# Zeros for the first products, a split first load, and one inverse on VectorE instead of through DRAM

## The chip, the core and the metric

The kernel runs on one NeuronCore of a Trainium2 chip. Its engines are TensorE (PE; its weight loads are listed apart, as PEld), VectorE (DVE), ScalarE (ACT), GpSimd (POOL) and SyncE (SP), which here issues all DMAs. The metric is the time of one execution on the device in microseconds, the median of several runs.

## The reference

Attention with capped scores over 4 batch entries of 12 heads (448 tokens, 64 features per head), then a layer norm and two feed-forward blocks:

```python
scores = cap * np.tanh(scale * (q @ k.T) / cap)
attn = np.exp(scores - scores.max(-1)); attn /= attn.sum(-1) + 1e-09
x = attn @ v                                # to [4, 448, 768]
xn = (x - mu) / np.sqrt(var + 1e-06) * g_ln
x = x + np.maximum(xn @ w_ch1, 0.0) @ w_ch2 # 768 -> 3072 -> 768
h = np.maximum(x @ w_in, 0.0); u, v = h[..., :512], h[..., 512:]
out = (u * (w_spatial @ norm(v) + b_spatial)) @ w_out
```

All is float32. The change touches only the attention of the first two batch entries.

## The kernel before

Every operation is recorded first. `Recorder` notes engine, a cost and a latency from a small table, and the call (line 560; the call itself is line 561, so almost every instruction of the profile bears L561). `Program.order` derives due times from TensorE's own order, and `Program.plan` is a list scheduler: it runs the recorded operations against those costs, gives out the buffers of the pools, and lets ScalarE take some of VectorE's copies where that is earlier. What it puts out is, for each engine, one fixed list, and each engine works through its list in order. So an operation that waits holds up all behind it on its engine, and SyncE's list holds up every DMA behind one that waits.

Heads are worked in pairs, named by the first head: pair i is heads i and i + 1 of the 48. The lead phase is the 12 pairs 0 to 22 of entries 0 and 1. For one pair:

- `emit_load(i)` loads `qk`, 128 rows (64 features of two heads) by 896: 448 query columns, then 448 key columns. There are two such buffers, so pair i + 4 is loaded over pair i.
- `lead_s(i)` makes three products of 128 keys by 448 queries into PSUM (`two`, `two`, `t3`), and ScalarE the tanh of each (scale `qsc`, made from the loaded `cap`) and the exponentials `e`. `lead_st(i)` does the last 64 keys of two pairs at once.
- `lead_v(i)` adds the exponentials up on VectorE (`es`), multiplies `e` with the values `vt` on TensorE into a `bank` of PSUM (there are only two in this phase), copies the result to `x`, and makes the row sums with products by ones (`onesr`, `sel`) in a bank.
- The row sums are inverted. `invert` (line 1001) takes a copy of them, writes it to DRAM (`sum`), reads it back spread over 128 rows (`rc`), inverts that on VectorE, writes it to DRAM (`inv`) and broadcasts it to a tile `hs` by two or four DMAs. For a pair named in `FAST` (line 938), VectorE inverts the bank directly, in four pieces of 112 columns. Pairs 8, 10, 20 and 22 have sums of their own; the others share them by two, and their DMAs bear the number of the second.
- `emit_n(i)` multiplies `x` by the inverse and `x_done` adds it to `acc`. After pair 10, the last of entry 0, `ln_mean` needs `acc`: a product `bank<-wh,onesr` for the mean over features.

Beside this, four rows of the first weight matrix are made ready (`make`): they are loaded as 64-bit words (`w`), put together by four operations into `wr`, split into two parts for the later products (`rs`, `wh`), and written to DRAM (`kept_w`).

Ahead of the recorded list TensorE multiplies zeros with zeros, into a bank that nothing reads.

Of the kernel before, what the change touches and what calls it, by code (L numbers as in the profile page):

```python
# [10 lines left out]
F32 = mybir.dt.float32  # L11
# [29 lines left out]
LN_AT = 4.2  # L41
MAKE = 3.1

FAST = 22,

COUNTS = 16, 10, 3, 2, 3, 1
FIRST = 2, 2, 2, 1
# [521 lines left out]
def attn_ffn_gmlp_kernel(  # L569
# [15 lines left out]
    nc = tc.nc  # L585
    prog = Program(nc)
    V, A, P, T, SP = (prog.engines[n] for n in ("V", "A", "P", "PE", "D"))
    B, H = qk.shape[0], qk.shape[1]
    KD, S = out.shape[1], out.shape[3]
# [70 lines left out]
    for stage in four, mid:  # L660
# [4 lines left out]
    xts = [[const.tile([128, S], F32, name=f"x{i}_{k}") for k in range(KD)] for i in range(2)]  # L665
# [3 lines left out]
    capt = const.tile([128, 1], F32, name="capt")  # L669
# [6 lines left out]
    banks = Slots("bank", [psum.tile([128, 512], F32, name=f"bank{i}") for i in range(2)],  # L676
                  late=[Later(f"bank{i}", [128, 512], F32) for i in range(2, 4)])
# [144 lines left out]
    def emit_load(i):  # L822

        if i >= len(heads):
            return
        b, h = heads[i]
        t = raws[i] = qks.get()

        SP.dma_start(out=t, in_=qk[b, h:h + 2].rearrange("a p n -> (a p) n")[64:192])

    def place(i):


        return slice(64, 128) if i // 2 % 2 else slice(0, 64)

    def emit_load_v(i):


        if i >= len(heads):
            return  # L840
        b, h = heads[i]
        u = raws["v", i] = vts[i // 2 % 2].get()
        p = place(i)
        SP.dma_start(out=u[:, 0:384].rearrange("p (a n) -> p a n", a=2),
                     in_=v[b, h:h + 2, :, 0:3].rearrange("a p c d -> p a (c d)"))
        SP.dma_start(out=u[p, 384:512].rearrange("p (a n) -> p a n", a=2),
                     in_=v[b, h:h + 2, p, 3].rearrange("a p d -> p a d"))
# [58 lines left out]
    def lead_v(i):  # L906
# [30 lines left out]
        R = [hs.get() for _ in now]  # L937
        if i in FAST:

# [104 lines left out]
    def emit_v(i, ns=range(4)):  # L1044
# [41 lines left out]
        R = [hs.get() for _ in now]  # L1086
        if i in FAST:

# [348 lines left out]
    def gmlp(bs, nxt):  # L1437
        for b in nxt:
            ln_load(b)
        if not last_pass[0]:  # L1440
            for i in range(1, KH):
                ahead("wu", i)
        vs = v_mm(range(2 * S // 128))
        for b in nxt:
            ln_mean(b)
        if last_pass[0]:
            mix_y()
            u_four(bs, 0)
            v_norm(vs)
            u_four(bs, 1)  # L1450
        else:
            u_units(bs, 0)
            v_norm(vs)
            for i in range(1, KH):
                for k in range(max(2 * i - 2, 0), 2 * i):
                    ahead("wo", k)
                u_units(bs, i)
        ysp.clear()
        sp = spatial()
        with prog.early():  # L1460
            for b in nxt:
                centre(b)
        for b in nxt:
            scale(b)
        bias = xts[0][KD - 1] if last_pass[0] else bsg.get()
        SP.dma_start(out=bias, in_=b_sp)
        for i in range(0, KH, 2):
            sp_pair(bs, (i, i + 1), sp, bias)
            if i + 2 == KH:
                with prog.early():  # L1470
                    for b in nxt:
                        normalise(b)
        us.clear()
        vn.clear()
        if last_pass[0]:
            o_four(bs)
            gs.clear()
            return
        for dts in ([0, 1, 2], *([dt] for dt in range(3, KD))):
            w = [weight("wo", dt) for dt in dts]  # L1480
            for b in bs:
                if b % 2:
                    for dt, x in zip(dts, w):
                        o_units(b, dt, [x])
                else:
                    o_units(b, dts[0], w)
        gs.clear()
        if nxt:
            for k in range(KD // 2):
                mix(k)  # L1490
        for b in nxt:
            ln_load(b)
# [209 lines left out]
    def second_pass(bs):  # L1702
        hidden.clear()
        for i in range(NF // 2):
            h_four(i)
        y_seven(wq, wq)
# [120 lines left out]
    def drive(units, todo):  # L1827

        todo = deque(sorted(todo, key=lambda t: t[0]))
        spent = 0  # L1830
        for n in units:
            spent += n
            while todo and todo[0][0] < spent:
                _, fn, args = todo.popleft()
                fn(*args)
        for _, fn, args in todo:
            fn(*args)

    def attend(first, n, per):
        todo = []  # L1840
        for j in range(0, n, 2):
            i = first + j
            t = per * j

            stages = [(S_AT[0] if i >= 2 * SPLIT else 0.0, emit_s, i, (0, 1)),
                      (S_AT[1] if i >= 2 * SPLIT else 0.1, emit_s, i, (2,)), (LOAD_QK, emit_load, i + 4),
                      (LOAD, emit_load_v, i + 2)]
            if i < 2 * H:

                stages = [(0.0, lead_s, i), (2.05, lead_v, i)] + stages[2:]  # L1850
            else:
                stages += [(2.05, emit_v, i)]
            if i // 2 % 2 == 0:
                stages += [(LEAD_ST, lead_st, i) if i < 2 * H else (ST, emit_st, i)]
            if alone(i):
                stages += [(4.2, emit_n, i)]
            elif i // 2 % 2:
                stages += [(4.2, emit_n, i - 2), (4.2, emit_n, i)]
            todo += [(t + x * per, fn, a) for x, fn, *a in stages]
        return todo  # L1860

    def main():
        with prog.at_once():
            emit_load(0)
            SP.dma_start(out=capt, in_=cap)
            emit_load(2)
            emit_load_v(0)
        SP.dma_start(out=g_t, in_=g_ln)
        P.memset(sel, 0.0)
        for j in (0, 2):  # L1870
            P.memset(sel[place(j), j // 2], 1.0)
        P.memset(ones32, 1.0)
        V.tensor_copy(onesr, ones32[:, 0:1].broadcast_to([128, 128]))
        P.memset(mhalf, -0.5)
        V.reciprocal(qsc, capt)
        V.tensor_scalar(out=qsc, in0=qsc, scalar1=float(D) ** -0.5, scalar2=None, op0=ALU.mult)

        lead = attend(0, 2 * H, 1.0) + [(x, fn, (b,)) for x, b in ((H + LN_AT, 0), (2 * H + 2.25, 1)) for fn in (ln_mean, ln_center)]
        lead += [(MAKE + j * H / EARLY, make, ("w1", j)) for j in range(EARLY)]
        drive([], lead)  # L1880
        for p in range(NP):
            bs = 2 * p, 2 * p + 1

            if p:
                last_pass[0] = True
                second_pass(bs)
                gmlp(bs, [])
                continue
            total = NF * 2 * 3 * KD
            rows = [("w2", (q, g)) for q in (BLOCKS[0], BLOCKS[2]) for g in range(NG)]  # L1890
            later = [("wv", k) for k in range(KD)] + [("wu", i) for i in range(1)] + [("wo", k) for k in range(0)]
            todo = [(total * (AFTER[0] + (AFTER[1] - AFTER[0]) * j / len(rows)), ahead, x) for j, x in enumerate(rows)]
            n = 2 * H
            drive(h_units(bs), todo + attend(n, n, AFTER[2] * total / n))
            raw6[:] = w6m, wcm, w6m
            y_seven(wqm, wqs, later)
            raw6[:] = w6g, wcg, w6g
            gmlp(bs, [2 * p + 2, 2 * p + 3])

    main()  # L1900
    tops.begin()
    att.begin()
# [4 lines left out]
    with tc.manual_schedule():  # L1907
        t = tok_t[0][0]
        nc.vector.memset(t[:], 0.0)
        nc.scalar.activation(out=t[:], in_=t[:], func=ACTF.Tanh)  # L1910
        t = xts[0][0]
        nc.vector.memset(t[:], 0.0)
        for _ in range(2):
            nc.tensor.matmul(out=banks.tiles[-1][:, 0:S], lhsT=t[:, 0:128], rhs=t[:], start=True, stop=True)
        prog.issue()


# [52 lines left out]
```

## Time and profile before

| | |
|---|---|
| runs | 1012.73, 1012.03, 1009.84 us; median 1012.03 |
| profiled execution | 1010.37 us, its span 1008.6 us |
| TensorE busy | 997.3 us (99%), 5108 instructions |
| VectorE busy | 855.2 us (85%) |
| ScalarE busy | 584.9 us (58%) |
| granted TensorE clock | 1.0 over the span |

The profile is one execution. Times in it count from the span's start. An engine's row gives, in brackets, how long the engine was idle just before and what ended that; a matmul's end is modelled, and a DMA's row on SyncE is its issue, not its transfer. SyncE's name in rows is SPq.

### The profile page before, as it was taken

What the parts mean: (1) busy time and instruction counts of PE and PEld (TensorE: products, weight loads), DVE (VectorE), ACT (ScalarE), POOL (GpSimd) and SP (SyncE); (2) the same over time, 40 slices, a digit from 0 to 9 for tenths busy, and PEclk for the clock granted to TensorE, in tenths of its full rate; (3) what the DMA queues carried; (4) which work ended last, traced back from release to release, by engine and by line L of the source; (5) the groups of instructions that cost most, each with busy time, mean ns of one, the idle gap of its engine ahead of it and who ended that gap; (6) DMA issues with size and microseconds to landing.
All of it is one profiled execution on the core that took longest, in us unless ns stands there. A gap on an engine that the chain in (4) does not pass through costs nothing.

```text
span 1008.6 us, 14721 instructions
## 1 busy us (share of the span) xinstructions
PE 997.3 (99%) x5108; PEld 827.7 (82%) x5108; DVE 855.2 (85%) x1425; ACT 584.9 (58%) x890; POOL 16.7 (2%) x22
## 2 busy tenths in 40 slices
PE   8999999999999999999999999999999999999998
PEld 2334787787788899998989889999999999998987
DVE  6767887888967899989889999877788988968996
ACT  7996955877775358656356355444453543314653
POOL 0000000000000000000000200000000000000010
PEclk9999999999999999999999999999999999999999
DMA  7546678988897998997386233565699857302402
GB/s 251 170 137 180 214 254 294 365 305 303 300 331 230 347 359 297 332 345 273 119 308 218 43 144 116 169 204 191 236 329 371 290 184 233 103 21 71 128 21 110
DMA packets 121197, 224.30 MB, mean 222 GB/s; under 512 B 20594, under 2 KB 83236, under 8 KB 121124
## 3 DMA queue, kind: packets, MB, share of 16 engines
q1 hardware_dynamic: 121124, 223.38, 65.1%
q8 instruction: 40, 0.66, 0.3%
q14 instruction: 33, 0.27, 0.1%
HBM read 152.76 MB, written 70.57 MB: 221 GB/s over the span
## 4 chain that ended last, share of the span: by engine, by line
PE 84%; DMA 6%; DVE 6%; issue 1%; ACT 1%; SPq 1%; DVEq 0%; ACTq 0%
PE bank L561 58%; PE two L561 26%; DMA w6m<-in_w_dram 2%; DVE rs L561 1%; DVE x L561 1%; DMA hs<-inv 1%; DMA std<-var_t 1%; DVE wh L561 1%; DMA w<-in_w_dram 1%; SPq L561 1%; PE t L561 1%; DVE qkg L561 1%; DMA wq<-kept_w 1%; DMA qk<-in_qk_dram 1%; DVE wr L561 1%
## 5 line engine op out<-in xcount | busy, mean ns | idle before, releaser
L561 PE MATMUL bank<-rs,wh 128*128 128x448 f32 x1728 | 362.9, 363 | 1.2 <-DVE rs L561 0.7
L561 PEld LDWEIGHTS bank<-rs,wh 128*128 128x128 f32 x1728 | 322.5, 187 | 29.5 <-issue 3.0
L561 PE MATMUL two<-rs,wh 128*128 128x448 f32 x462 | 103.7, 362 | 0.7 <-DVE wh L561 0.7
L561 DVE TENSOR_TENSOR rs<-hs,rs 128x448 fp32r<-128x448 f32 x159 | 94.3, 618 | 4.7 <-ACT rs L561 4.5
L561 ACT ACTIVATE rs<-hs 128x448 fp32r<-128x448 f32 x135 | 73.2, 570 | 32.7 <-DMA hs<-h 31.4
L561 PEld LDWEIGHTS two<-rs,wh 128*128 128x128 f32 x462 | 86.5, 187 | 6.9 <-DVE wh L561 1.0
L561 DVE TENSOR_TENSOR wh<-wr,wh 128x768 fp32r<-128x768 f32 (+2 forms) x66 | 57.4, 871 | 3.0 <-ACT wh L561 2.5
L561 ACT ACTIVATE hs<-bank 128x448 f32<-128x448 f32 x58 | 31.5, 543 | 40.1 <-PE bank L561 33.9
L561 ACT ACTIVATE wh<-wr 128x768 fp32r<-128x768 f32 (+2 forms) x44 | 33.7, 766 | 30.8 <-PE bank L561 16.6
L561 ACT ACTIVATE es<-es,capt 128x896 f32<-128x896 f32 x42 | 42.6, 1052 | 0.1
L561 ACT ACTIVATE hx<-bank 128x448 f32<-128x448 f32 x30 | 16.3, 543 | 39.2 <-PE bank L561 30.1
L561 PE MATMUL two<-qk 64*128 64x448 f32 (+1 forms) x168 | 36.1, 575 | 2.9 <-DMA qk<-in_qk_dram 2.0
L561 ACT ACTIVATE rs<-x 128x448 fp32r<-128x448 f32 x29 | 16.3, 575 | 36.5 <-DVE x L561 35.1
L561 PE MATMUL bank<-es,vt 128*64 128x448 f32 (+1 forms) x192 | 36.0, 551 | 0.0
L561 ACT ACTIVATE es<-two,qsc 128x896 f32<-128x896 f32 x32 | 31.5, 1007 | 6.3 <-PE two L561 6.3
L561 PE MATMUL two<-wh,rs 128*128 128x512 f32 x144 | 34.7, 389 | 0.0
L561 PE MATMUL bank<-rx,whb 128*128 128x448 f32 x144 | 32.7, 362 | 0.0
L561 PE MATMUL two<-rx,whb 128*128 128x448 f32 x144 | 32.7, 362 | 0.0
L561 DVE TENSOR_TENSOR es<-es,es 128x896 f32<-128x896 f32 x24 | 26.1, 1086 | 7.5 <-ACT es L561 7.5
L561 PEld LDWEIGHTS two<-qk 64*128 64x128 f32 (+1 forms) x168 | 11.3, 173 | 25.5 <-issue 9.1
L561 PEld LDWEIGHTS two<-wh,rs 128*128 128x128 f32 x144 | 27.0, 188 | 5.6
L561 ACT ACTIVATE e<-e,capt 128x2688 f32<-128x2688 f32 (+1 forms) x14 | 31.0, 2224 | 0.2
(268 smaller groups left out, 1966.1 us busy)
## 6 DMA issues: line engine op xcount, KB each, us to landing
hs<-h SPq DMA_DIRECT2D x168, 224.0 KB
h<-hx SPq DMA_DIRECT2D x84, 224.0 KB
w<-in_w_dram SPq DMA_DIRECT2D x24, 768.0 KB
qk<-in_qk_dram SPq DMA_DIRECT2D x24, 448.0 KB
h<-hs SPq DMA_DIRECT2D x48, 224.0 KB
kept_w<-wr SPq DMA_DIRECT2D x24, 384.0 KB
w6q<-in_w_dram SPq DMA_DIRECT2D x12, 768.0 KB
w6m<-in_w_dram SPq DMA_DIRECT2D x12, 768.0 KB
```

The source lines that it names most:

```text
L561: fn(*(put(a) for a in args), **{k: put(a) for k, a in kw.items()})
```

## The change

`FAST` names pair 10 too, so its row sums are inverted on VectorE, in four pieces, and its five DMAs, the copy and the small reciprocal are gone. The first `qk` tile comes in two DMAs, the queries with the first 128 keys and then the other keys, with `cap` between them. The products of zeros read a constant of the runtime's that GpSimd fills before the program's start, in place of a tile that VectorE set to zero; a third product of 112 columns follows the two of 448.

```diff
-FAST = 22,
+FAST = 10, 22
...
-        SP.dma_start(out=t, in_=qk[b, h:h + 2].rearrange("a p n -> (a p) n")[64:192])
+        x = qk[b, h:h + 2].rearrange("a p n -> (a p) n")[64:192]
+        for r in (slice(0, S + 128), slice(S + 128, 2 * S)) if i == 0 else (slice(0, 2 * S),):
+            SP.dma_start(out=t[:, r], in_=x[:, r])
+            if r.start == 0 and i == 0:
+                SP.dma_start(out=capt, in_=cap)
...
             emit_load(0)
-            SP.dma_start(out=capt, in_=cap)
             emit_load(2)
...
-        t = xts[0][0]
-        nc.vector.memset(t[:], 0.0)
-        for _ in range(2):
-            nc.tensor.matmul(out=banks.tiles[-1][:, 0:S], lhsT=t[:, 0:128], rhs=t[:], start=True, stop=True)
+        zeros = nc.const_aps.tensor(0.0, [128, S], F32)
+        for n in (S, S, S // 4):
+            nc.tensor.matmul(out=banks.tiles[-1][:, 0:n], lhsT=zeros[:, 0:128], rhs=zeros[:, 0:n], start=True, stop=True)
```

The planner then orders the lists anew. TensorE's list stays the same but for the zeros; those of VectorE, ScalarE and SyncE differ in places up to the layer norm of entry 0, and are the same after it. (Numbers at the end of a name are tile numbers, which shift by two after the change.)

In SyncE's list the load of the keys of pair 6 and the third weight load change places, so that the keys go first. Pair 10's five DMAs are gone from it.

VectorE at the additions for pair 2 (`es_434<-e_420` before, `es_432<-e_418` after). Before:

```order
L561 TENSOR_SCALAR wr_92<-w_424 128x768
L561 CAST rs_65<-wr_93 128x768
L561 TENSOR_TENSOR es_434<-e_420 128x896
L561 TENSOR_TENSOR rs_66<-wr_93,rs_65 128x768
L561 TENSOR_TENSOR es_434<-es_434,e_420 128x896
L561 COPY x_1_114<-bank_139 128x448
```

and after:

```order
L561 TENSOR_SCALAR wr_92<-w_422 128x768
L561 TENSOR_TENSOR es_432<-e_418 128x896
L561 CAST rs_65<-wr_93 128x768
L561 TENSOR_TENSOR es_432<-es_432,e_418 128x896
L561 TENSOR_TENSOR rs_66<-wr_93,rs_65 128x768
L561 COPY x_1_114<-bank_139 128x448
```

The subtraction into `rs_66` moved behind the second addition.

SyncE behind the last write of a prepared weight row, `kept_w_3` (the sums and inverses of pairs 0 and 2 bear a 2, those of 4 and 6 a 6). Before:

```order
L561 DMA sum_2_143<-hs_79 4x448
L561 DMA vt_0_415<-in_v_dram 64x2x64
L561 DMA vt_0_415<-in_v_dram 128x2x192
L561 DMA rc_89<-sum_2_143 128x14
L561 DMA qk_412<-in_qk_dram 128x896
L561 DMA sum_6_146<-hs_80 4x448
L561 DMA inv_2_144<-rc_89 128x14
L561 DMA qk_413<-in_qk_dram 128x896
L561 DMA rc_90<-sum_6_146 128x14
L561 DMA hs_79<-inv_2_144 64x448 x2
L561 DMA hs_81<-inv_2_144 64x448 x2
L561 DMA inv_6_147<-rc_90 128x14
```

and after, behind the same write:

```order
L561 DMA vt_0_413<-in_v_dram 64x2x64
L561 DMA vt_0_413<-in_v_dram 128x2x192
L561 DMA sum_2_143<-hs_79 4x448
L561 DMA sum_6_146<-hs_80 4x448
L561 DMA qk_410<-in_qk_dram 128x896
L561 DMA rc_89<-sum_2_143 128x14
L561 DMA rc_90<-sum_6_146 128x14
L561 DMA qk_411<-in_qk_dram 128x896
L561 DMA inv_2_144<-rc_89 128x14
L561 DMA inv_6_147<-rc_90 128x14
L561 DMA hs_79<-inv_2_144 64x448 x2
L561 DMA hs_82<-inv_2_144 64x448
```

Two value loads moved ahead of the first sums, the two chains of sums now go side by side, and both inverse writes stand ahead of the first broadcast.

SyncE around the load of pair 16's keys, the first `qk` of each piece (the second is pair 18's). Before:

```order
L561 DMA hs_82<-inv_8_150 64x448
L561 DMA sum_10_151<-hs_84 2x448
L561 DMA qk_412<-in_qk_dram 128x896
L561 DMA hs_82<-inv_8_150 64x448
L561 DMA rc_89<-sum_10_151 128x7
L561 DMA qk_413<-in_qk_dram 128x896
L561 DMA inv_10_152<-rc_89 128x7
L561 DMA hs_84<-inv_10_152 64x448 x2
```

and after:

```order
L561 DMA hs_81<-inv_8_150 64x448 x2
L561 DMA qk_410<-in_qk_dram 128x896
L561 DMA qk_411<-in_qk_dram 128x896
L561 DMA vt_0_412<-in_v_dram 128x2x192
L561 DMA vt_0_412<-in_v_dram 64x2x64
```

Pair 10's chain is gone from between the loads, and pair 16's keys now stand behind both rows of pair 8's broadcast.

## Rows read from the trace of the kernel before

**Rows 1.** The page's first part, of the whole span: busy us, share, instructions.

```profile
PE 997.3 (99%) x5108; PEld 827.7 (82%) x5108; DVE 855.2 (85%) x1425; ACT 584.9 (58%) x890; POOL 16.7 (2%) x22
```

**Rows 2.** The waits of TensorE up to 112 us: total us, times, longest.

```profile
PE two L561 <- DMA qk<-in_qk_dram: 2.0, 2, 1.0
```

**Rows 3.** The timeline of TensorE, 16 to 75 us: start and length in us.

```profile
20.11 0.97 PE L561 MATMUL two<-qk 64*64 64x448 f32 x4 [1.01 <-DMA qk<-in_qk_dram]
...
24.37 0.96 PE L561 MATMUL bank<-es,onesr 128*32 128x448 f32 x8
...
36.10 0.96 PE L561 MATMUL bank<-es,onesr 128*32 128x448 f32 x8
...
45.97 1.34 PE L561 MATMUL bank<-es,vt 64*64 64x448 f32 x8
...
59.71 1.02 PE L561 MATMUL two<-qk 64*128 64x448 f32 x4 [1.01 <-DMA qk<-in_qk_dram]
...
60.66 0.98 PE L561 MATMUL bank<-es,vt 64*64 64x448 f32 x8
...
68.76 1.01 PE L561 MATMUL bank<-wh,onesr 128*128 128x448 f32 x2 [0.46 <-DVE x L561]
```

**Rows 4.** The timeline of VectorE, up to 75 us.

```profile
10.50 0.56 DVE L561 TENSOR_SCALAR wr<-w 128x768 f32<-128x768 f32 x1 [5.34 <-DMA w<-in_w_dram]
...
22.31 0.95 DVE L561 TENSOR_TENSOR rs<-wr,rs 128x768 fp32r<-128x768 f32 x1
...
23.18 1.09 DVE L561 TENSOR_TENSOR es<-es,e 128x896 f32<-128x896 f32 x1
...
33.92 0.95 DVE L561 SCALAR_TENSOR_TENSOR wr<-w,wr 128x768 int32<-128x768 int32 x1
...
34.79 1.08 DVE L561 TENSOR_TENSOR es<-es,e 128x896 f32<-128x896 f32 x1
...
45.72 0.56 DVE L561 COPY hs<-bank 128x448 f32<-128x448 f32 x1
...
60.03 0.63 DVE L561 TENSOR_TENSOR x<-x,hs 128x448 f32<-128x448 f32 x1 [2.49 <-DMA hs<-inv]
```

**Rows 5.** Two stretches: engines' busy us, granted clock, DMA share and GB/s.

```profile
5.00:10.00 5.00, 5.00 (x28) 1.69 (x28) 0.15 (x1) 3.91 (x5) 0.00 (x0) 1.00 1.04 350
...
20.00:30.00 10.00, 9.89 (x56) 3.15 (x56) 9.96 (x14) 9.40 (x10) 0.00 (x0) 1.00 0.73 240
```

**Rows 6.** The timeline of the first microseconds.

```profile
1.41 3.35 PE L1914 MATMUL bank<-x 128*128 128x448 f32 x4 [1.41 <-DVE x L1912]
...
4.69 2.06 PE L561 MATMUL two<-qk 64*128 64x448 f32 x8
...
6.05 1.01 ACT L561 ACTIVATE e<-two,qsc 128x896 f32<-128x896 f32 x1 [3.83 <-PE two L561]
```

**Rows 7.** The chain of waits up to 110 us: start, us, what.

```profile
14.58 5.49 DMA qk<-in_qk_dram
...
55.73 4.21 DMA hs<-inv
...
60.79 1.82 DMA inv<-rc
```

**Rows 8.** The timeline of SyncE's DMA issues.

```profile
34.90 0.33 SPq L561 DMA_DIRECT2D kept_w<-wr  x1
...
35.28 0.61 SPq L561 DMA_DIRECT2D sum<-hs  x1
...
46.10 0.59 SPq L561 DMA_DIRECT2D inv<-rc  x1
...
49.23 0.54 SPq L561 DMA_DIRECT2D rc<-sum  x1
...
55.34 0.34 SPq L561 DMA_DIRECT2D qk<-in_qk_dram  x1
```

**Rows 9.** VectorE's groups by form: busy us, mean ns, idle before.

```profile
L561 DVE RECIPROCAL hs<-bank 128x112 f32<-128x112 f32 x4 | 3.1, 813 | 0.7 <-PE bank L561 0.7
```

## The prediction

> **What bounds the kernel now.** Read the page's first part, then the waits of TensorE, then its timeline up to 75 us. TensorE is busy for 997.3 us, 99% of the span [rows 1]: only its idle time and its slow stretches can be won. Nearly all of that idle lies ahead of 70 us, in the attention of the first two batch entries: two waits for query/key tiles, 2.0 us together [rows 2], and one for the normalised output. From there on the waits are four of 0.3 to 0.7 us, which this change doesn't touch, and the order shows no row that moves after the first hundred or so on any engine. So I sum what TensorE gains up to about 70 us and carry that to the end.
>
> The waits stand in TensorE's timeline [rows 3]: 1.01 us before 20.11, 1.01 before 59.71, 0.46 before 68.76. A fourth is hidden in a duration: the eight passes at 45.97 take 1.34 us where the eight at 60.66 take 0.98, because their second half writes the bank that VectorE empties from 45.72 to 46.28 [rows 4].
>
> Two other engines are close behind. VectorE is busy 9.96 of 10 us from 20 to 30 [rows 5], and the row sums at 24.37 and 36.10 [rows 3] start 0.10 and 0.23 us after VectorE's additions end (23.18 + 1.09 and 34.79 + 1.08, [rows 4]). What TensorE gains before those points it keeps only as far as VectorE gives those additions earlier.
>
> **The change part by part.**
>
> Products of zeros, first queries. Before, four passes on zeros start at 1.41 and take 3.35 us; the first scores follow at 4.69 and the first tanh at 6.05 [rows 6]. Now the products need no memset of VectorE's and start some 0.6 us earlier; a quarter product is added, by its columns a quarter of half of those 3.35, 0.4 us. That ends them at about 4.5 (1.41 - 0.6 + 3.35 + 0.4), and by then 295 KB of the first tile are asked for instead of 459. So the first tanh may come 0.1 to 0.6 us earlier. None of it reaches the end: VectorE's work starts with the weight load that lands at 10.50 [rows 4] and is then nearly gapless, and the sums at 24.37 wait for VectorE. That load's place among the bytes is the same; one more issue ahead of it (about 0.45 us of SyncE) lies beside a DMA queue that is full by then. I take 0, bounds -0.4 (the weights come that much later) to +0.4.
>
> The wait at 20.11. The tile was issued at 14.58, behind a 768 KB weight load, and took 5.49 us [rows 7]. Now it goes ahead of that load (order, SyncE). 786 KB at the 350 GB/s of [rows 5] are 2.2 us, so it lands at about 17.9 and the 1.01 goes. But at 24.37 VectorE rules: one subtraction, 22.31 to 23.18, now stands behind the addition, so the sums come 0.87 us earlier, not 1.01. Between there and 36.10 VectorE's list swaps one cast for one multiply of like length and puts one 0.87 us operation behind (33.92 to 34.79) for the one it took on: again 0.87. Bounds 0.5 to 1.0.
>
> The hidden wait at 45.97. VectorE's copy of pair 8's sums stood behind the reciprocal of pair 6, whose input had to come back from DRAM. Pair 6's sums are now copied by ScalarE and written ahead of a key load, so that reciprocal is some 2 us earlier: 1.34 - 0.98 = 0.36 gained, bounds 0 and 0.36. TensorE is then 1.23 ahead.
>
> The wait at 59.71, the term that decides. Those keys (pair 16) were issued at 55.34 [rows 8] and came just before 59.71, 4.3 us later. The removal takes away five DMAs of pair 10, and the next key load, which stood behind a wait for one of them, moves up by about 1.5 us; but that one is needed only after 67. The load TensorE waits for stood behind the first broadcast of pair 8 and one sum write; now behind both broadcasts. So it is as early as pair 8's inverse, a chain of three DRAM trips on SyncE's queue. I follow that queue. The last weight write, 34.90 before, waits for the operation put behind the addition: 36.0. Two value loads now stand ahead of the first sums: 37.6 instead of 35.28. Then sums of pair 6, keys, two reads, keys, two inverse writes: the broadcasts start near 44.5. Against that, the second inverse is written before them, where before SyncE stood until 46.10 for it, some 1.4 us. With 0.6 us for each issue the read of pair 8's sums comes at 49.3 (49.23 before), and the keys at about 55.5. Landing in the same 4.3 us, up to 0.37 us more for the second broadcast ahead or 0.6 less for fewer transfers around it, they come between 59.1 and 60.2; I take 59.5, near the old row. TensorE waits about 2 us here, and the 1.23 it had won is spent. Gain at this point 0.2, bounds -0.5 and +0.7.
>
> The wait at 68.76. Pair 10's multiply waited for its inverse broadcast. Four reciprocals at 0.81 us [rows 9] on VectorE, from about 57 to 60, replace it; 2.49 us before 60.03 VectorE stood idle there [rows 4]. The statistics product is then no longer late: 0.46 gained. If the cover goes, the reciprocals hold a PSUM bank until 60.2 that TensorE next writes 1.4 us after the keys arrive, near 60.9.
>
> **Sum.** 0.2 + 0.46 = about 0.7 us against the profiled execution's 1010.37, so 1009.7 there; that execution lies 1.7 us under the median 1012.03 of the runs shown. Against the median: 1011.3. The terms' bounds give -0.1 to 1.2; with the -0.4 and +0.4 of the start, the likeliest case's own range is 1010.4 to 1012.5.
>
> **The rivals.**
>
> A, all four waits go (chance 0.22). The keys come in time if SyncE reaches them a microsecond earlier and they land faster. 459 KB at 350 GB/s [rows 5] are 1.3 us, and a bare round trip took 1.82 [rows 7]: 3.1 instead of 4.3. From 54.4 that is 57.5, just when TensorE arrives (58.70 - 1.23). Then 0.87 + 0.36 + 1.01 + 0.46 = 2.7, time 1009.3. For it: SyncE's 1.4 us stand before 46.10 goes, and one sum write and one read leave the stretch. Against it: the broadcast issued at 55.73 took 4.21 us in the same stretch [rows 7], so transfers are slow there.
> The Trainium skill (DMA: Bandwidth & Descriptors, "Anatomy of one DMA") gives a fixed 2.0 us or so and bytes over 436 GB/s, 3.05 us for these keys by its fit for the other issue path; the row here has 4.3. By the page, with the issue at 55.5, the keys would come at 58.6 and the sum would be 1.6 instead of 0.7.
>
> B, slower (chance 0.13). One mechanism: pair 8's inverse comes later, because the weight write and the two value loads ahead of the first sums cost SyncE 2.3 us (35.28 to 37.6) and the 1.4 us before 46.10 are not won back. Then the keys are issued near 56.9 and land at 61.2; 1.5 lost, 0.46 won: 1013.1. It decides from an issue later than 55.8. For it: the order shows it plainly. Against it: the chain is not one of busy time, it has idle in it.
>
> C, the reciprocals bind (chance 0.05). If the multiplies ahead of them wait for broadcasts until 58.5, the bank comes free at 61.8, 0.9 late: 1011.8.
>
> **How the numbers follow.** The forecast case has 0.60. What a measurement of this kernel can tell from no change is 0.3%, 3.0 us, and the runs shown span 2.9. Faster by more takes A with luck (half of 0.22), and a tenth of the forecast case: 0.20. Slower by more needs a median above 1015.1, a third of B and a little of the rest: 0.07. Same: 0.73. The range goes from a little under A, 1009.0, to B, 1013.1.
>
> **What would show it.** Right: the first key wait in TensorE's list gone; the sums at 23.5 and 35.2; the eight passes near 45 at 0.98; a wait of about 2 us for pair 16's keys, TensorE going on at 59 to 60; no wait before the statistics product. Wrong: that key wait under 1 us (A), or TensorE going on after 60.3 (B), or a wait for a reciprocal (C); or any wait after 75 us that was not there.

## The result, and the profile after

The changed kernel takes 1017.38 us (median of 6 runs, 1015.14 to 1021.02), the kernel before, run beside it, 1011.81 us (6 runs). The ratio is 1.0051, with a 95% interval of 1.0033 to 1.0069: slower. Forecast were 1011.3 us and a range up to 1013.1. The profiled execution took 1015.29 us, its span is 1013.5 us, 4.9 us above that of before.

TensorE's work is as long as before (the first row answers to [rows 1]), and the waits up to 112 us hold the loss (columns as in [rows 2]):

```profile
PE 998.5 (99%) x5110; PEld 828.9 (82%) x5110; DVE 859.1 (85%) x1428; ACT 583.8 (58%) x888; POOL 17.0 (2%) x22
```

TensorE's waits:

```profile
PE two L561 <- DMA qk<-in_qk_dram: 5.3, 3, 4.0
PE bank L561 <- DVE x L561: 1.1, 1, 1.1
```

Of the 5.3 us for keys 4.0 are one wait. The other two are 0.38 us at 5.95, for the second piece of the split load, and 0.96 at 14.61, where before waited 0.9 us for ScalarE. TensorE's timeline, the places of [rows 3]:

```profile
4.42 1.15 PE L561 MATMUL two<-qk 64*128 64x448 f32 x4
...
23.76 0.57 PE L561 MATMUL bank<-es,onesr 128*32 128x448 f32 x2 [0.20 <-DVE es L561]
...
45.35 0.98 PE L561 MATMUL bank<-es,vt 64*64 64x448 f32 x8
...
56.39 2.48 PE L561 MATMUL bank<-e,vt 128*64 128x448 f32 x12 [1.08 <-DVE x L561]
62.86 1.86 PE L561 MATMUL two<-qk 64*128 64x448 f32 x4 [4.00 <-DMA qk<-in_qk_dram]
64.66 1.70 PE L561 MATMUL bank<-es,vt 64*64 64x448 f32 x8
...
72.95 0.68 PE L561 MATMUL bank<-wh,onesr 128*128 128x448 f32 x2
```

Set instruction against instruction, the difference between the two executions builds up like this. At 46 us the changed kernel is 0.98 us ahead. A wait of 1.08 us at 56.39, which before did not have, makes that 0.16 behind. The wait for pair 16's keys is 4.00 us in place of 1.01: 3.16 behind. The products after it run slowly (1.70 us for eight passes that took 0.98 before): 4.72 behind at 66.29. The statistics product no longer waits: 3.86 behind at 73.56. Over the other 940 us 1.0 us more is lost: 4.9.

The slow products are the granted clock. In windows of the changed kernel it is the third number from the end of a row:

```profile
59.00:61.00 2.00, 0.00 (x0) 0.00 (x0) 2.00 (x4) 1.29 (x1) 0.00 (x0) 1.00 0.67 192
...
62.80:63.50 0.70, 0.64 (x2) 0.53 (x4) 0.70 (x2) 0.00 (x0) 0.00 (x0) 0.50 0.73 262
...
67.00:68.00 1.00, 1.00 (x7) 0.20 (x3) 0.00 (x0) 0.64 (x1) 0.00 (x0) 1.00 0.06 13
```

At the end of TensorE's wait the clock fell from 1.00 to 0.50, that is from 2.4 to 1.2 GHz, and it was back at 1.00 near 66. All six runs of the changed kernel have a mean granted clock under 1 (0.994 to 0.998).

Why the keys came so late is read from SyncE, to be set beside [rows 8]:

```profile
36.22 0.33 SPq L561 DMA_DIRECT2D kept_w<-wr  x1
...
37.95 1.23 SPq L561 DMA_DIRECT2D sum<-hs  x2
39.27 0.38 SPq L561 DMA_DIRECT2D qk<-in_qk_dram  x1
...
40.94 0.38 SPq L561 DMA_DIRECT2D qk<-in_qk_dram  x1
43.04 1.13 SPq L561 DMA_DIRECT2D inv<-rc  x2
46.76 1.78 SPq L561 DMA_DIRECT2D hs<-inv  x3
...
51.70 0.54 SPq L561 DMA_DIRECT2D rc<-sum  x1
...
58.41 1.51 SPq L561 DMA_DIRECT2D qk<-in_qk_dram  x2
```

The kernel before, at the load ahead of its first inverse, at that inverse and at its broadcast:

```profile
38.75 0.33 SPq L561 DMA_DIRECT2D qk<-in_qk_dram  x1
...
40.80 0.33 SPq L561 DMA_DIRECT2D inv<-rc  x1
...
42.84 3.21 SPq L561 DMA_DIRECT2D hs<-inv  x4
```

In the changed kernel the first inverse is written at 43.04, and the first broadcast, which waits for that write to land, goes out 3.72 us later; before, it was 2.04 us (40.80 to 42.84). The list of waits, for SyncE from 36 to 60 us, says what it stood for (total, times, longest):

```profile
SPq L561 <- DVE wr L561: 4.1, 1, 4.1
SPq L561 <- DMA inv<-rc: 3.0, 2, 2.6
```

From there on everything on SyncE is 2 to 3 us late against before, the read of pair 8's sums at 51.70 (49.23 before) and pair 16's keys at 58.41 (55.34). The chain of waits of the changed kernel has the rest (start, us, what):

```profile
52.29 2.79 DMA hs<-inv
...
55.17 1.17 DVE x L561 x2
...
58.41 4.32 DMA qk<-in_qk_dram
```

The 1.08 us ahead of 56.39 have the same cause: VectorE's copy that frees the bank stood behind a multiply that waited for a broadcast issued at 52.29.

### The profile page after: what moved, and what is told of

The parts are those of the page before. It is cut to its first block, busy times and chain, and to the rows that moved or that the text cites. A ratio compares the mean times of both kernels' runs of the same rounds, so it can differ in the third digit from the quotient of the medians.

```text
span 1013.5 us, 14715 instructions
## 1 busy us (share of the span) xinstructions
PE 998.5 (99%) x5110; PEld 828.9 (82%) x5110; DVE 859.1 (85%) x1428; ACT 583.8 (58%) x888; POOL 17.0 (2%) x22
## 4 chain that ended last, share of the span: by engine, by line
PE 79%; DVE 9%; DMA 7%; ACT 2%; issue 2%; SPq 1%; DVEq 0%; ACTq 0%
PE bank L561 55%; PE two L561 24%; DMA w6m<-in_w_dram 2%; DVE rs L561 2%; DVE x L561 2%; DMA std<-var_t 1%; DMA hs<-inv 1%; DVE es L561 1%; DVE wh L561 1%; DVE wr L561 1%; DMA inv<-rc 1%; SPq L561 1%; DMA w<-in_w_dram 1%; DVE qkg L561 1%; DMA hs<-std 1%
```

## The experiments

Ratios are to the kernel before on the same chip, with 95% intervals. They ran in groups on one chip each: e1 to e4, e5 to e8, e9 to e11; the kernel before had medians of 1009.95, 1010.68 and 1011.21 us there. In the edits called MOVES the planner's lists stay as they are, and a few DMAs are then moved in SyncE's list alone: a line names a DMA, how many of its kind come ahead of it, and behind or before which other it goes. `qk_8` is pair 16's keys, `qk_7` pair 14's, `sum_0_2_`, `rc_0` and `inv_0_2_` the first chain, `inv_0_8_` pair 8's inverse, `kept_w1_3_` the last weight write.

**Which part of the change makes it.**

e1, FAST alone:

```diff
-FAST = 22,
+FAST = 10, 22
```

> The kernel before with pair 10 added to FAST and nothing else: zeros and first load as before. SyncE's list then has the sums' chains side by side as after the change, VectorE's list up to 40 us is that of before. Theory Q (the loss is made in SyncE's queue: chains side by side, so pair 8's inverse and pair 16's keys are issued 3 us late): a wait of 3 to 5 us for pair 16's keys, the granted clock down behind it, 1016 to 1019 us. Rival L (the split first load and the order of VectorE's list that came with it make the loss): no such wait, 1010 to 1012 us.

Measured: 1014.74 us, ratio 1.0046 (1.0029 to 1.0063). TensorE's timeline:

```profile
62.79 1.86 PE L561 MATMUL two<-qk 64*128 64x448 f32 x4 [4.46 <-DMA qk<-in_qk_dram]
```

SyncE's:

```profile
34.49 0.33 SPq L561 DMA_DIRECT2D kept_w<-wr  x1
...
36.26 2.41 SPq L561 DMA_DIRECT2D sum<-hs  x2
...
42.57 0.80 SPq L561 DMA_DIRECT2D inv<-rc  x2
46.31 1.78 SPq L561 DMA_DIRECT2D hs<-inv  x3
...
58.21 1.00 SPq L561 DMA_DIRECT2D qk<-in_qk_dram  x2
```

The weight write is as early as before, and still the first broadcast goes out 3.74 us after the inverse and the keys at 58.21. With the chains side by side neither the split load nor the late weight write is needed for the loss; theory L falls.

e2, the rest without FAST:

```diff
-FAST = 10, 22
+FAST = 22,
```

> The changed kernel without pair 10 in FAST: its inverse goes through DRAM again. SyncE's list still has the chains side by side. Theory Q: keys of pair 16 issued near 57.5 to 58.5, a wait of 3 to 4 us for them, 1015 to 1018 us. Rival V (VectorE's four reciprocals and the bank they hold make the loss): no wait over 1 us for keys, 1010 to 1012 us.

Measured: 1015.42 us, ratio 1.0045 (1.0029 to 1.0061). TensorE's timeline:

```profile
63.18 1.42 PE L561 MATMUL two<-qk 64*128 64x448 f32 x4 [3.62 <-DMA qk<-in_qk_dram]
```

Here the keys go out at 58.74 although there are no reciprocals, and although they stand ahead of pair 8's second broadcast again, as before; theory V falls. Each of the two edits makes the planner put the chains side by side, and together they cost no more than each alone.

e8, the zeros alone:

```diff
-        t = xts[0][0]
-        nc.vector.memset(t[:], 0.0)
-        for _ in range(2):
+        zeros = nc.const_aps.tensor(0.0, [128, S], F32)
+        for n in (S, S, S // 4):
...
```

> The kernel before with the products of zeros of the changed kernel and nothing else; all lists behind them are those of before. All theories here expect no difference: first scores 0.3 us earlier, VectorE's start set by the weight load as before, 1009 to 1011 us, ratio within 0.2% of 1.

Measured: 1009.18 us, ratio 0.9982 (0.9965 to 0.9999), at the edge of no difference; its profile has no row that shows where 1.8 us would come from, and I don't claim them.

**What in SyncE's list makes it.**

e3, pair 16's keys four places up:

```diff
+MOVES = (('qk_8<-', 0, 'behind', 'inv_0_8_', 0),)
```

> The changed kernel with one DMA moved in SyncE's list: pair 16's keys from behind pair 8's two broadcasts to directly behind the write of pair 8's inverse (four places up). Issue then near 54.7, landing near 59.0. Theory Q: the wait of 4.0 us goes to under 1 us and the granted clock stays at 1.0 (1.5 us more); VectorE's reciprocals, done at 62.3, may then hold a bank for up to 2 us: 1011 to 1014 us. Rival V: the reciprocals set the end of the stretch whatever the keys do, so a wait for the bank of 3 us or more takes the place of the wait for keys: 1016 to 1018 us.

Measured: 1013.97 us, ratio 1.0035 (1.0019 to 1.0050). TensorE's timeline:

```profile
55.37 2.48 PE L561 MATMUL bank<-e,vt 128*64 128x448 f32 x12 [0.49 <-DVE x L561]
58.63 1.02 PE L561 MATMUL two<-qk 64*128 64x448 f32 x4 [0.78 <-DMA qk<-in_qk_dram]
...
61.35 1.61 PE L561 MATMUL bank<-es,vt 64*64 64x448 f32 x4 [0.80 <-DVE hs L561]
```

Its windows, columns as in [rows 5]:

```profile
60.00:65.00 5.00, 4.20 (x14) 1.38 (x12) 5.00 (x9) 1.39 (x3) 0.00 (x0) 0.65 0.29 92
65.00:70.00 5.00, 5.00 (x20) 1.21 (x20) 1.76 (x3) 4.81 (x4) 0.00 (x0) 0.66 0.02 3
```

The wait for keys went to 0.78 as theory Q has it, and a bank held by the reciprocals costs 0.80, less than V wants. But the clock fell all the same, and here it cost more than the waits: TensorE is 0.67 us ahead of before at 60.01 and 3.97 behind at 68.42, of which 0.80 is the wait. Of the 12 runs the four with a mean clock of 1.0 took 1009.5 to 1012.9 us, the eight below it 1013.4 to 1017.3. My expectation of a clock at 1.0 was wrong.

e4, the chains of the first sums back in the order of before:

```diff
+MOVES = (
+    ('sum_0_2_', 0, 'before', 'vt1__2<-', 0),
+    ('rc_0<-', 0, 'before', 'qk_6<-', 0),
+    ('sum_0_6_', 0, 'behind', 'qk_6<-', 0),
+    ('inv_0_2_', 0, 'behind', 'sum_0_6_', 0),
+    ('qk_7<-', 0, 'behind', 'inv_0_2_', 0),
...
```

> The changed kernel with SyncE's list put back to the order of before from the last weight write to pair 8's sums and the broadcasts of pair 6 (nine DMAs moved); everything else, pair 16's keys behind both broadcasts too, stays. Theory Q with the place I now give it (the chains of the first sums): first broadcast near 43 instead of 46.8, keys issued near 55.5, wait for them 1.5 to 2.5 us, clock at 1.0: 1010.5 to 1012.5 us. Rival K (only the place of the keys behind both broadcasts counts, not the sums): keys issued near 58, wait near 4 us, 1016 to 1018 us.

Measured: 1013.28 us, ratio 1.0026 (1.0012 to 1.0039). SyncE's timeline:

```profile
37.43 0.34 SPq L561 DMA_DIRECT2D kept_w<-wr  x1
...
42.39 0.33 SPq L561 DMA_DIRECT2D inv<-rc  x1
...
44.78 3.10 SPq L561 DMA_DIRECT2D hs<-inv  x4
...
57.94 1.09 SPq L561 DMA_DIRECT2D qk<-in_qk_dram  x2
```

In the old order the first broadcast follows the inverse by 2.39 us instead of 3.72. But the keys are late again, because the weight write, for which VectorE is later, came at 37.43 in this run (34.90 before, [rows 8]; 36.22 in the changed kernel, above all since VectorE stood 0.85 us for a weight load here), and the old order hands that 2.5 us on one to one. So there are two causes and each alone makes the keys late: the order of the chains (e1), and the weight write that stands ahead of them (e4). They don't add up: e1 has the weight write 1.73 us earlier than the changed kernel and the keys only 0.20 us earlier, since SyncE waits there for the second pair of sums (the two issues take 2.41 us) and for the inverse. Theory Q was half of it. K had the issue right (57.94), but for another reason than the keys' own place, and not the wait, 1.27 us, nor the time.

The keys are not all that e4 loses by. TensorE has a second wait there, the hidden one of 45.97 in a larger form: VectorE's copy of pair 8's sums stands again behind a reciprocal that waits for DRAM.

```profile
48.71 0.97 PE L561 MATMUL bank<-es,vt 64*64 64x448 f32 x4 [1.29 <-DVE hs L561]
```

And this profile is not typical of the run: it is one of two executions of twelve with a mean clock of 1.0, and took 1010.85 us against the median of 1013.28. What the other ten lose is not shown.

e6, the first sums ahead of the weight write:

```diff
+MOVES = (
+    ('sum_0_2_', 0, 'before', 'kept_w1_3_', 0),
+    ('rc_0<-', 0, 'before', 'kept_w1_3_', 0),
+)
```

> The changed kernel with two DMAs of SyncE moved: the first sums (pairs 0 and 2) and their read back go ahead of the last write of a prepared weight row, for which SyncE stood 4.1 us while these sums had lain ready since 27.1. Theory H (SyncE's list stands behind that write, and VectorE makes it late): the chains start 3 us earlier or more, the first broadcast is issued at 45 or before instead of 46.8, pair 16's keys before 57, their wait falls from 4.0 to under 2.5 us: 1011 to 1014 us. Rival T (the transfers behind the two key loads set the chains, not their issue): keys again near 58.4 and 1016 to 1018 us.

Measured: 1011.18 us, ratio 1.0010 (0.9991 to 1.0029). SyncE's timeline:

```profile
31.77 0.62 SPq L561 DMA_DIRECT2D sum<-hs  x1
...
40.70 2.76 SPq L561 DMA_DIRECT2D inv<-rc  x2
44.81 1.77 SPq L561 DMA_DIRECT2D hs<-inv  x3
...
56.13 1.00 SPq L561 DMA_DIRECT2D qk<-in_qk_dram  x2
```

Two DMAs moved, and most of the loss is gone. The wait for the keys, 2.92 us, shrank less than I wrote, because TensorE came earlier too: the one at 56.39 is gone. The clock still falls behind it; eleven of the twelve runs have a mean under 1.0.

e9, the inverses ahead of pair 14's keys:

```diff
+MOVES = (
+    ('inv_0_2_', 0, 'before', 'qk_7<-', 0),
+    ('inv_0_6_', 0, 'before', 'qk_7<-', 0),
+)
```

> The changed kernel with one key load moved in SyncE's list: pair 14's keys (458,752 bytes) from ahead of the two first inverse writes to behind them. Theory D (the inverse writes took 3.71 and 3.07 us because they were queued behind that load's data, not because they were issued late): they land in 2 to 2.5 us as the row of before did (1.97 us), the first broadcast is issued 1.5 us earlier or more (45.2 or before, 46.8 in the changed kernel), pair 16's keys near 57, their wait near 2.5 us: 1 to 3 us faster than the changed kernel, ratio to before about 1.003. Rival I (they are slow for their own sake, 7,168 packets of few bytes side by side, or because two go at once): landing again 3 us or more behind the issue, keys near 58.4, ratio 1.005.

(The 7,168 in this text are the bytes of one inverse write.) Measured: 1014.78 us, ratio 1.0044 (1.0026 to 1.0062). SyncE's timeline:

```profile
42.41 0.80 SPq L561 DMA_DIRECT2D inv<-rc  x2
43.30 1.18 SPq L561 DMA_DIRECT2D qk<-in_qk_dram  x1
45.15 1.78 SPq L561 DMA_DIRECT2D hs<-inv  x3
...
56.59 1.00 SPq L561 DMA_DIRECT2D qk<-in_qk_dram  x2
```

The first broadcast now follows the inverse by 2.74 us instead of 3.72, and before it was 2.04. That goes the way of theory D, but the key load is not all of it.

The packets in the traces, the single pieces that the DMA engines move, show what else there was. Before, the 128 packets of the write ran from 41.63 to 42.02, just as the data of the key load issued at 38.75 ended (41.73), and the broadcast went out 0.82 us behind them. In the changed kernel 240 of the 256 packets of the two writes ran from 44.16 to 44.93, at the end of the second key load's data (44.68). The last 16 started at 45.68, when a packet of 16 KB on the queue that the profile calls "instruction" ended (44.37 to 45.69); they were through at 45.89, and the broadcast followed 0.87 us later. In e1, e2 and e5 16 packets are held back by such a packet in the same way. In e9 the writes ran from 43.23 to 44.29, the last of them too behind such a packet (43.14 to 44.08); before, it came at 44.72, when the first write was long done. So of the 1.68 us by which the trip is longer than before, about 1.0 is this collision (44.93 to 45.89). Without the packets that were held back, the trip from the issue to the last one is 1.22 us before, 1.50 in e9 and 1.89 in the changed kernel: 0.4 for the key load (theory D) and 0.3 for two writes at once (theory I). Each is one execution, and no run takes the instruction packet away.

The wait for keys, 3.32 us, and the time moved less than expected; against the changed kernel the time can't be told apart, and the profile is that of the fastest of the eight runs.
The Trainium skill (DMA: Bandwidth & Descriptors, "Two DMAs through the same engine are not ordered") says that within one queue of a DMA engine descriptors start in order. These runs agree as far as they go: in both kernels the packets of the write come at the end of the data of the load ahead of it.

**What the clock costs.** e5, TensorE kept busy with zeros during the wait:

```diff
+            def fill():
+                for _ in range(5):
+                    nc.tensor.matmul(out=two.place(), lhsT=zeros[:, 0:128], rhs=zeros, start=True, stop=True)
...
+            prog.ops[i][0][k][3].insert(0, fill)
```

> The changed kernel with five products of zeros (448 columns, into the tile that the scores then overwrite) put into TensorE's list ahead of pair 16's scores, to keep TensorE busy in the 4.0 us in which it waits for the keys; they compute nothing. Theory C (part of the loss is the granted clock, which falls behind that wait): the clock stays at 1.0 there, the products behind it take the full-speed time, 1.5 us less than the changed kernel in a profile, so 1014 to 1016 us on the scale of the first runs. Rival W (the wait alone makes the loss, the clock costs nothing that isn't made up): no change, 1017 us; if the zeros outlast the wait, above that.

Measured: 1013.65 us, ratio 1.0035 (1.0019 to 1.0052). TensorE's timeline, and the window that it falls in:

```profile
63.26 1.02 PE L561 MATMUL two<-qk 64*128 64x448 f32 x4 [0.67 <-DMA qk<-in_qk_dram]
```

```profile
60.00:65.00 5.00, 4.33 (x19) 1.46 (x17) 5.00 (x8) 0.67 (x1) 0.00 (x0) 1.00 0.56 203
```

The scores start as late (63.26), their four passes take 1.02 us instead of 1.86, and nine of ten runs have a mean clock of 1.0. The 1.56 us behind the wait are the clock. The time fits theory C; its interval overlaps that of the changed kernel, so the rows carry this, not the medians.

**A better version.** e7, both moves of e6, the first inverse ahead of pair 14's keys, and the keys of e3:

```diff
+MOVES = (
+    ('sum_0_2_', 0, 'before', 'kept_w1_3_', 0),
+    ('rc_0<-', 0, 'before', 'kept_w1_3_', 0),
+    ('inv_0_2_', 0, 'before', 'qk_7<-', 0),
+    ('qk_8<-', 0, 'behind', 'inv_0_8_', 0),
+)
```

> As the run with the sums first, and two more moves in SyncE's list: the first inverse is written ahead of the keys of pair 14, and pair 16's keys go directly behind the write of pair 8's inverse. Theory H: broadcasts from 44 on, keys of pair 16 issued near 53 and there before TensorE wants them, multiplies and reciprocals on VectorE done by 60, so no wait over 0.7 us between 45 and 70 and the clock at 1.0: 1007 to 1010 us, faster than both. Rival B (VectorE is full by 60 whatever SyncE does, as in the run with the keys early alone): a wait for a bank of 0.8 us or more stays, the clock falls, 1012 to 1015 us.

Measured: 1008.60 us, ratio 0.9979 (0.9966 to 0.9991). SyncE's timeline at pair 16's keys, then TensorE's:

```profile
52.80 0.34 SPq L561 DMA_DIRECT2D qk<-in_qk_dram  x1
```

```profile
59.98 0.97 PE L561 MATMUL bank<-es,vt 64*64 64x448 f32 x4 [0.49 <-DVE hs L561]
```

That last is TensorE's only wait between 20 and 70 us. It is faster than both kernels: 0.2% against before, and by the two ratios (0.9979 over 1.0051) 0.7% against the changed kernel. But e8, the zeros alone on the same chip, has 0.9982 and a median of 1009.18 us, so the runs don't show that the split load, pair 10 in `FAST` and the four moves together bring anything over the zeros.

e10 and e11 take one edit out of it, with the same four moves: e10 the split load (`emit_load` and the place of `cap` as before), e11 pair 10 in `FAST`.

> The run with the sums first and the keys early, but with the first load in one piece as before (the zeros and pair 10 in FAST stay, and the same four moves on SyncE). The wait for the keys at 20.11 is then there again, VectorE's list up to 40 us is that of before. If VectorE's additions bound that stretch anyway, the time is that of the run with the split within 0.5 us: ratio to before 0.997 to 0.999. If the split load brings its full 1 us, it is 1 us slower than that run: ratio 0.998 to 1.000.

Measured: 1009.59 us, ratio 0.9985 (0.9972 to 0.9997). The wait for keys near 20 is back (1.07 us), and the time is that of e7 within its interval. The ratio lies in both ranges that were expected, so it decides nothing; TensorE's rows do. At the score products that start at 37.04 in e7 and at 37.56 here, e7 is 0.52 us ahead, half of the 1.07: so far VectorE bounds it, as the prediction had it. The rest is lost where both wait for the bank that the reciprocals hold: the score products behind it start at 60.88 in e7 and at 60.44 here. In these two profiles the split load brings nothing to the end.

> The run with the sums first and the keys early, but pair 10's inverse goes through DRAM again (zeros and split load stay, the same four moves on SyncE). If the four reciprocals on VectorE are worth something once SyncE's queue is mended: a wait before the statistics product near 68 of 0.5 to 2 us, ratio to before 0.998 to 1.001. If they cost more by the bank they hold (0.49 us in that run) than they save: ratio 0.996 to 0.998.

Measured: 1011.77 us, ratio 1.0000 (0.9985 to 1.0016). TensorE's timeline:

```profile
70.00 1.01 PE L561 MATMUL bank<-wh,onesr 128*128 128x448 f32 x2 [3.40 <-DVE x L561]
```

With the queue mended, the inverse through DRAM is what TensorE waits for, 3.40 us: pair 10 in `FAST` is worth about 0.2% there (the intervals of e7 and e11 just overlap, so the row carries this), and the bank that it holds costs 0.49 us.

## Why the prediction was wrong

- **Products of zeros, first queries: right.** First scores at 4.42 (4.69 before), nothing of it at the end. The weight load came to VectorE at 10.83 instead of 10.50, inside the bounds.
- **The wait at 20.11: right in kind.** It is gone, and the sums wait for VectorE (0.20 at 23.76). 0.62 us were kept at 36 instead of 0.87; the later weight load is the difference.
- **The hidden wait at 45.97: right.** 0.98 us for the eight passes, and a lead of 0.98 (forecast 1.23).
- **Pair 16's keys: the step that failed.** The sentence is "the broadcasts start near 44.5". I had followed SyncE's list issue by issue, and right so far (sums at 37.95 for 37.6), but from there to the first broadcast I allowed 6.9 us. Before, that stretch took 7.56 us (35.28 to 42.84), and the new order made it longer, 8.81 (37.95 to 46.76): the reads and the inverse writes stand among 459 KB key loads in the same queue, and the write of the inverse alone kept the first broadcast for 3.72 us instead of 2.04, about 1.0 of the difference by a packet of the instruction queue that no list orders. The broadcast started at 46.76, 2.3 us later than forecast; the read of pair 8's sums came at 51.70 for 49.3, the keys were issued at 58.41 for 55.5. Their own 4.3 us were right (4.32). The Trainium skill (DMA: Bandwidth & Descriptors, "Anatomy of one DMA") makes 3.05 us an estimate for them, by its fit for the other issue path; that was not seen here.
- **Two prices were missing behind it.** The late broadcasts hold a copy on VectorE and with it a bank (1.08 us at 56.39): I followed the queue to the keys only. And a wait of 4 us lowers the granted clock, 1.56 us: the sum has no term for it, since no row of before shows the clock under 1.00, and I took a longer wait to cost its own length. The bounds of the term went to keys that land at 60.2; they landed at 62.73.
- **The wait at 68.76: right.** No wait there, and no reciprocal was waited for (rival C stayed hidden behind the keys; e3 and e7 show it, 0.80 and 0.49 us; its price should have been 1012.2 by its own 0.9 us on top of 1011.3, not 1011.8).
- **Rival B was nearest**, with the right place and the right sign for the point from which it decides (an issue later than 55.8). It had the issues ahead of the first sums, but not the longer trips behind them. Its chance was 0.13, and its price had 1.5 us less in issue than came, without the wait at 56.39 and the clock; that is why even the range missed. I set against it that the chain had idle in it; e4 shows that it has none to give where it begins, at the weight write.

The 1.0 us lost after 75 us stays open. It is made of waits that are 0.36 us at 113.81, 0.42 at 259.72 and 1.23 at 402 to 404, less 0.72 and 0.28 that before had at 466.84 and 762.73. The lists are the same there; the profiles of e3, e6 and e7 lack the waits near 402, those of e2 and e10 have them.

## What to carry to other kernels

In a queue that works in order, price a small dependent transfer by what stands ahead of it in the data as well as by its issue, and ask of each waiting entry at the head of the list whether anybody behind it could go first: here SyncE stood 4.1 us for one write of a prepared weight, which nobody needed soon, with the first sums of a chain of three trips ready behind it, and moving two DMAs ahead of it took most of the loss away (e6). Where a planner makes the lists, an edit's own saving can be smaller than what its new order does, so read the lists of every engine up to the next wait, and try the edit with the old order and the old lists with the edit. And when a late transfer is priced, add what TensorE's clock does after the wait.

## What the runs showed of the hardware

The granted clock fell in e3 although no wait of TensorE was longer than 0.80 us: 0.49, 0.78 and 0.80 us lay between 54.9 and 61.4, the clock was at 0.50 from 62.0 to 68.0 (read in windows of half a microsecond), and it cost 3.8 us. In the kernel before, single waits of 1.01 and 0.46 us left it at 1.00, and in e4 two of 1.29 and 1.27 us, 14 us apart. Several short waits close together can thus be dearer than one.

A small write can be held up by a transfer that stands in no list: in the changed kernel, e1, e2 and e5 a 16 KB packet of the instruction queue kept the last 16 of 256 packets 0.9 to 1.1 us behind the others, and the broadcast behind them waited for those.
